# One queue for K and V, and a part of w2 on 64 partitions in eight small transfers

## The chip, the cores and the metric

The kernel runs on one core of a Trainium2 chip. The metric is the device time of the whole program in microseconds (us). Next to it stands the span of one profiled execution, from the first to the last event that the hardware profiler recorded on that core.

The engines of a core have short names here: PE multiplies matrices (PEld loads its weights), DVE and ACT work on vectors and activations, POOL on general operations, SP only issues transfers. "SPq" and "ACTq" are the instruction queues of SP and ACT where they issue a DMA.

## The reference, cut to what matters

One decode step of two branches on the same normalised input, for two sequences (B = 2, one token each, D = 448):

```python
xn = layernorm(x)
q = (xn @ wq) -> 16 heads of 256
k, v = the last 4096 rows of 8 kv heads, each used by 2 query heads
p = softmax(q . k * 256 ** -0.5)
attention = (p . v) @ wo
h = xn @ w1 + b1                                  # 1792 hidden values
dense = (h * tanh(softplus(h))) @ w2
out = x + attention + dense
```

All tensors are bf16. For each pair of a kv head and a sequence, 2 MB of K and 2 MB of V are read once: 64 MB of K and V in all. wq is 3.7 MB, wo 3.7 MB, w1 and w2 1.6 MB each.

## The kernel before

A "head" below is one of the 16 pairs (kv head, sequence); `heads[i]` lists them. The main loop runs over `i` from 0 to 17 and is a software pipeline: at step i it loads K of head i+2 and V of head i, computes the scores of head i, and the values of head i-2 (`KA = 2`).

A K tile holds 128 partitions with 32 key rows each. `turn(s)` (L364) transposes half a K tile on DVE, `scores(s)` (L376) multiplies it on PE with the query block `qdiag`, ACT takes the exponential (L386), `turn_p(s)` (L397) transposes the probabilities on DVE. `values(i)` (L431) multiplies them with V; the last four heads use `values_fixed(i)` (L479), 64 small matmuls per head. `scale_o` (L447) divides by the denominator. After each second head `mix` projects the pair with its slice of wo through `add` (L214) into an accumulator that lives in PSUM to the end. The output is cast by DVE and ACT (L562) and written by one transfer (L563).

The dense branch rides along: `load_dense` loads w1 (L275) and w2 (L280) near the start, `dense_in` computes the hidden values at step 0 (L290, bias L299) and their activation, `dense_out` projects them through w2 at step 1. With 896 hidden values per half of w1 and 128 partitions, there are NF = 7 columns of hidden values for each half. The hidden value number q x 7 + c of a half lies on partition q in column c. b1 has a tile of its own, loaded at the start by ACT.

Queues: SP issues wq, w1, w2, all K tiles, all wo slices, V of the last two heads and the output. ACT issues x, b1 and V of heads 0 to 13. Each engine issues its instructions in program order (`issue_in_order`), a DMA among them; a V load on ACT thus stands between ACT's exponentials.

Buffers: K has 4 tiles, V 5, wo 3. The two parts of wq, w1 and w2 use V tiles before V does. K of head i+2 can be loaded once K of head i-2 has been transposed, V of head i once the values of head i-5 are computed. Besides, the program has eight semaphores for its transfers, used in turn over both queues, and a transfer waits for the one that had its semaphore before.

In the names of the profile, `k`, `v`, `kt`, `pT`, `wo`, `psA` are these tiles; `v` also stands for wq, w1 and w2 in V tiles.

Of the kernel before, what the change touches and what calls it, by code (L numbers as in the profile page):

```python
# [11 lines left out]
BF16 = mybir.dt.bfloat16  # L12
# [22 lines left out]
def kernel(  # L35
# [13 lines left out]
    nc = tc.nc  # L49
    P = 128  # L50
    Q = 32
    NQ = P // Q

    Bsz, Sq, D = A_x.shape
# [6 lines left out]
    F = B_w1.shape[1]  # L61
    T = W // P
    NH = 2
    TH = T // NH
    NX = 2
    NS = D * NX // P
    HW = HqDh // NX
    HF = F // NX
    HH = Hq // NX
    NF = HF // P  # L70
    ND = Dh // P
    NB = Dh // (2 * Q)
    NE = 2
# [13 lines left out]
    consts = ctx.enter_context(tc.tile_pool(name="consts", bufs=1))  # L87
# [8 lines left out]

    x_bf = consts.tile([Bsz, D], BF16)
    nc.scalar.dma_start(out=x_bf[:, :], in_=A_x.flatten_outer_dims())
    b1_sb = consts.tile([1, F], BF16)
    nc.scalar.dma_start(out=b1_sb[:, :], in_=B_b1.rearrange("(o f) -> o f", o=1))  # L100


    def v_tile(n):
        t = v_pool.tile([P, T * Dh], BF16, tag="v", name="v")
        return t[:, 0:n]
# [6 lines left out]
    for lo, hi in ((0, SC), (SC, NS)):  # L112
        w = v_tile((hi - lo) * HW).rearrange("p (s n) -> p s n", n=HW)
# [17 lines left out]
        out=rstd[:], in_=mv[:, 1:2], func=ACT.Sqrt, bias=eps_t[:], scale=1.0  # L131
# [5 lines left out]
    for r in range(2):  # L137
        n = (NS + 1 - r) // 2
        nc.vector.tensor_scalar(  # L139
            out=xn_bf[:, r : NS : 2, :, :],  # L140
# [12 lines left out]
    for b4 in range(NB):  # L153
        rows = slice(b4 * Q, (b4 + 1) * Q)
        for j in range(NQ):
            nc.vector.tensor_copy(
                out=spread[rows, b4, j * Q : (j + 1) * Q], in_=ident[rows, rows]
# [3 lines left out]
    for j in range(1, NQ):  # L161
        nc.vector.tensor_tensor(
            out=hsel, in0=hsel, in1=ident[:, j * Q : (j + 1) * Q : HS], op=ALU.add
# [5 lines left out]
    for i in range(NW):  # L169
        t = consts.tile([P, NB * NE, P], BF16, name=f"qdiag{i}")  # L170
# [5 lines left out]
    for s in range(NS):  # L176
# [7 lines left out]
        out=odd[:],  # L184
        in_=ident[:].rearrange("p (u o) -> p o u", o=2),
# [4 lines left out]
    for par in range(2):  # L190
        for x in range(NX):
            which = (par + x) % 2
            nc.vector.tensor_scalar(
                out=xs[:, par : NS : 2, x, :],
# [14 lines left out]
    def part(n):  # L209
        return psA[n // 2][n * Q : n * Q + Bsz, :]  # L210

    def add(lhsT, w, start=False, stop=False):
        for n in range(NO):
            nc.tensor.matmul(  # L214
                part(n),
                lhsT=lhsT,
                rhs=w[:, n * DO : (n + 1) * DO],
                start=start,
                stop=stop,
                tile_position=(0, n * Q),  # L220
                skip_group_check=True,
            )
# [45 lines left out]


    act_bf = consts.tile([P, NF, NX, Bsz], BF16)  # L270
    dense = {}

    def load_dense():
        dense["w1"] = v_tile(NS * HF).rearrange("p (s n) -> p s n", s=NS)
        nc.sync.dma_start(  # L275
            out=dense["w1"],
            in_=B_w1.rearrange("r (x n) -> (r x) n", x=NX).rearrange("(p s) n -> p s n", s=NS),
        )
        dense["w2"] = v_tile(NX * NF * D).rearrange("p (x c d) -> p x c d", x=NX, c=NF)
        nc.sync.dma_start(  # L280
            out=dense["w2"], in_=B_w2.rearrange("(x q c) d -> q x c d", x=NX, q=P)
        )

    def dense_in():
        w1_v = dense.pop("w1").rearrange("p s (q c) -> p s c q", c=NF)
        b1_v = b1_sb[:].rearrange("o (x q c) -> o x c q", x=NX, c=NF)
        hT_ps = ps_m.tile([P, NF, NX, Bsz], FP32, tag="m", name="hT_ps")
        for c in range(NF):
            for s in range(NS):
                nc.tensor.matmul(  # L290
                    hT_ps[:, c, :, :].rearrange("p x b -> p (x b)"),
                    lhsT=w1_v[:, s, c, :],
                    rhs=xs[:, s, :, :].rearrange("p x b -> p (x b)"),
                    start=(s == 0),
                    stop=False,
                    skip_group_check=True,
                )
            for x in range(NX):
                nc.tensor.matmul(  # L299
                    hT_ps[:, c, x, :],  # L300
                    lhsT=b1_v[:, x, c, :],
                    rhs=ones[:, :],
                    start=False,
                    stop=True,
                    skip_group_check=True,
                )
        shape = [P, NF, NX, Bsz]
        h_sb = consts.tile(shape, FP32, name="h_sb")
        nc.vector.tensor_copy(out=h_sb[:], in_=hT_ps[:])
        u_sb = consts.tile(shape, FP32, name="u_sb")  # L310
        nc.scalar.activation(out=u_sb[:], in_=h_sb[:], func=ACT.Exp)
        t_sb = consts.tile(shape, FP32, name="t_sb")
        nc.vector.scalar_tensor_tensor(
            out=t_sb[:], in0=u_sb[:], scalar=2.0, in1=u_sb[:], op0=ALU.add, op1=ALU.mult
        )
        den = consts.tile(shape, FP32, name="den_sb")
        nc.vector.tensor_scalar(
            out=den[:], in0=t_sb[:], scalar1=2.0, scalar2=None, op0=ALU.add
        )
        nc.vector.reciprocal(out=den[:], in_=den[:])  # L320
        nc.vector.tensor_tensor(out=t_sb[:], in0=t_sb[:], in1=den[:], op=ALU.mult)
        nc.vector.tensor_tensor(out=act_bf[:], in0=h_sb[:], in1=t_sb[:], op=ALU.mult)

    def dense_out():
        w2_sb = dense.pop("w2")
        for x in range(NX):
            for c in range(NF):
                add(act_bf[:, c, x, :], w2_sb[:, x, c, :])


    NSTEP = len(heads) * NH
# [3 lines left out]
    def load_k(i):  # L335
        kvh, b = heads[i]
        t = k_pool.tile([P, T * Dh], BF16, tag="k", name="k")
        nc.sync.dma_start(  # L338
            out=t[:], in_=A_k_cache[b, kvh, s0:Sk, :].rearrange("(p t) d -> p (t d)", p=P)
        )  # L340
        k_t[i] = t

    def load_v(i, queue, cuts=(0, T)):
        kvh, b = heads[i]
        t = v_tile(T * Dh).rearrange("p (t d) -> p t d", t=T)
        vin = A_v_cache[b, kvh, s0:Sk, :].rearrange("(p t) d -> p t d", p=P)
        for lo, hi in zip(cuts, cuts[1:]):
            queue.dma_start(out=t[:, lo:hi, :], in_=vin[:, lo:hi, :])
        v_t[i] = t

    def load_wo(kvh, parts=1):
        w = wo_pool.tile([P, rep, ND * D], BF16, tag="wo", name="wo")
        r0 = kvh * rep * Dh
        win = A_wo[r0 : r0 + rep * Dh, :].rearrange("(h p c) d -> p h (c d)", h=rep, p=P)
        for u in range(parts):
            hs = slice(u * rep // parts, (u + 1) * rep // parts)
            nc.sync.dma_start(out=w[:, hs, :], in_=win[:, hs, :])
        wo_t[kvh] = w

    def turn(s):  # L360
        kt = kt_pool.tile([P, TH * Dh], BF16, tag="kt", name="kt")
        i, half = divmod(s, NH)
        k = k_t[i] if half < NH - 1 else k_t.pop(i)
        nc.vector.transpose(  # L364
            out=kt[:].bitcast(FP32),
            in_=k[:, half * TH * Dh : (half + 1) * TH * Dh].bitcast(FP32),
        )
        kt_t[s] = kt
# [131 lines left out]
    NK = len(heads)  # L500
    KA = 2

    load_k(0)
    load_dense()
    load_k(1)
    project()
# [5 lines left out]
    def close(i):  # L512
        if i < NK - NFIX:
            finish(i)
        kvh, b = heads[i]
        if b == Bsz - 1:
            mix(kvh)

    for i in range(NK + KA):
        if i + 2 < NK:  # L520
            load_k(i + 2)
        if i < NK:
            if i < NK - 2:
                load_v(i, nc.scalar)
            elif i < NK - 1:
                load_v(i, nc.sync)
            else:
                load_v(i, nc.sync, (0, T // 2, 3 * T // 4, T))
            kvh, b = heads[i]
            if b == Bsz - 1:  # L530
                load_wo(kvh, parts=1 if i < NK - 1 else 2)
            for half in range(NH):
                s = i * NH + half
                if s + 1 < NSTEP:
                    turn(s + 1)
                scores(s)
                if s >= 1:
                    turn_p(s - 1)
                if s == NSTEP - 1:
                    turn_p(s)  # L540
                if half == 0 and i > KA:
                    close(i - KA - 1)
            if i + 2 < NK:
                build_q(i + 2)
        if i == NK:
            close(i - KA - 1)
        if i == 0:
            dense_in()
        if i == 1:
            dense_out()  # L550
        if i >= KA:
            if i - KA < NK - NFIX:
                values(i - KA)
            else:
                values_fixed(i - KA)
        if i >= NK:
            close(i - KA)
# [37 lines left out]
```

The softmax here doesn't subtract the row's maximum and nothing guards it: scores larger than these inputs give would overflow.

## Time and profile before

| | us |
|---|---|
| three runs | 193.58, 194.19, 196.42 |
| median | 194.19 |
| the profiled execution's own time | 193.58 |
| its span | 191.8 |
| PE busy (share of the span) | 146.1 (76%) |
| DVE busy | 113.5 (59%) |
| ACT busy | 32.5 (17%) |
| POOL busy | 27.1 (14%) |

The transfers read 77.67 MB from HBM. SP's queue (q1) carried 48.30 MB, ACT's (q10) 29.37 MB; their packets took 59.8% and 35.8% of the time of 16 DMA engines.

How to read the views: the page cuts the span into 40 slices of 4.8 us and gives the busy share of each as a digit. A row of the timeline has start, duration, engine, line, operation, output and input, count, and in brackets how long the engine had been idle and what ended that. A row of the windows has the stretch, its length, then for each engine its busy time and the number of instructions, then the granted clock of PE, the mean busy share of the DMA engines, and GB/s.

DVE waits 45.2 us in all for K tiles (12 waits, the longest 8.7), which is its largest wait.

### The profile page before, as it was taken

To read this page: it belongs to the slowest core of one execution; us is meant where nothing else is said; L and a number is where in the kernel's file an instruction comes from. 1 tells how busy PE (TensorE), PEld (TensorE's weight loads), DVE (VectorE), ACT (ScalarE), POOL (GpSimd) and SP (SyncE) were. 2 spreads that over 40 slices of the span, in tenths; PEclk is the share of its full clock that TensorE was granted. 3 is DMA by queue.
4 is the path that set the end of the run, shared out by engine and by line. 5 is a ranking of instruction groups with operands and counts; after the bars stand their busy time and mean duration, and the time that the engine had idled before them with its cause. 6 is when DMAs were issued, how large, how long until landed. Compare 5 with 4: busy or idle time off the path is not lost.

```text
span 191.8 us, 2945 instructions
## 1 busy us (share of the span) xinstructions
PE 146.1 (76%) x1158; PEld 71.8 (37%) x1158; DVE 113.5 (59%) x195; ACT 32.5 (17%) x82; POOL 27.1 (14%) x139
## 2 busy tenths in 40 slices
PE   0104299389997089998997599978996699869893
PEld 0004238224443034353442243434352244326482
DVE  7800540699940575686923939393918575676731
ACT  2300011011222011122122111220221112211201
POOL 8000433003303002030302021300230030000000
PEclk9999999657999855999999969996999789997985
DMA  6999999999999999999999999999999999999940
GB/s 222 425 429 442 414 428 436 434 434 410 444 424 427 424 433 421 434 427 422 434 431 434 420 431 437 420 434 422 432 431 434 420 429 432 437 418 426 406 173 4
DMA packets 7816, 77.85 MB, mean 406 GB/s; under 512 B 758, under 2 KB 2810, under 8 KB 3323
## 3 DMA queue, kind: packets, MB, share of 16 engines
q1 hardware_dynamic: 5780, 48.30, 59.8%
q10 hardware_dynamic: 2022, 29.37, 35.8%
q8 instruction: 9, 0.15, 0.3%
q14 instruction: 5, 0.03, 0.0%
HBM read 77.67 MB, written 0.00 MB: 405 GB/s over the span
## 4 chain that ended last, share of the span: by engine, by line
DMA 68%; PE 18%; DVE 10%; SPq 1%; issue 1%; ACT 0%; ACTq 0%; DVEq 0%
DMA k<-in_A_k_cache_dram 54%; DMA v<-in_B_w_dram 14%; PE sc L376 9%; DVE kt L364 7%; PE o L431 4%; PE q L479 3%; DVE pT L397 1%; PE psA L214 1%; PE q L460 1%; PE den L414 1%; DVE oT L447 1%; SPq L114 0%; ACT p L386 0%; SPq L275 0%; SPq L338 0%
## 5 line engine op out<-in xcount | busy, mean ns | idle before, releaser
L364 DVE STREAM_TRANSPOSE kt<-k 128x2048 f32<-128x2048 f32 x32 | 73.4, 2295 | 45.2 <-DMA k<-in_A_k_cache_dram 45.2
L376 PE MATMUL sc<-kt,qdiag 128*128 128x512 bf16 x256 | 75.5, 446 | 17.7 <-DVE kt L364 17.0
L376 PEld LDWEIGHTS <-qdiag 128*128 128x128 bf16 x256 | 25.2, 107 | 58.8 <-issue 35.0
L431 PE MATMUL o<-v,pT 128*4 128x512 bf16 x192 | 43.6, 380 | 0.0
L264 POOL COPY qdiag<-qrep 32x8 bf16<-32x8 bf16 x128 | 23.1, 213 | 129.0 <-PE sc L376 109.4
L386 ACT ACTIVATE p<-sc 128x512 bf16<-128x512 f32 x32 | 19.1, 597 | 102.3 <-PE sc L376 100.3
L431 PEld LDWEIGHTS <-pT 128*4 128x4 bf16 x192 | 15.8, 87 | 22.0 <-issue 0.3
L397 DVE STREAM_TRANSPOSE pT<-p 128x512 bf16<-128x512 bf16 x32 | 21.5, 672 | 1.1 <-ACT p L386 1.1
L439 ACT COPY o_sb<-o 4x512 f32<-4x512 f32 x12 | 6.9, 574 | 36.7 <-PE o L431 36.7
L235 PE MATMUL qT_ps<-xs,v 128*128 128x4 bf16 x112 | 3.3, 166 | 9.7 <-DMA v<-in_A_wq_dram 6.9
L214 PE MATMUL psA<-wo,oT 128*2 128x112 bf16 x128 | 3.6, 249 | 8.9 <-DVE oT L447 8.9
L460 PEld LDWEIGHTS q<-ident_f,o_sb 4*128 4x128 f32 x48 | 6.6, 206 | 5.5 <-issue 5.5
L414 PEld LDWEIGHTS den<-sums,ones_f 128*128 128x128 f32 x32 | 6.8, 217 | 3.1 <-issue 1.3
L460 PE MATMUL q<-ident_f,o_sb 4*128 4x4 f32 x48 | 7.6, 261 | 0.0
L462 DVE COPY osum<-q 128x4 f32<-128x4 f32 x12 | 1.9, 159 | 9.4 <-PE q L460 9.4
L479 PEld LDWEIGHTS <-v 128*128 128x128 bf16 x256 | 7.4, 100 | 0.0
L479 PE MATMUL q<-pT,v 128*128 128x2 bf16 x256 | 7.2, 164 | 0.0
L235 PEld LDWEIGHTS <-v 128*128 128x128 bf16 x112 | 3.1, 104 | 9.9 <-DMA v<-in_A_wq_dram 7.0
L244 DVE CAST qT<-qT_ps 128x64 bf16<-128x64 f32 x1 | 0.2, 224 | 10.3 <-PE qT_ps L235 10.3
L386 ACT ACTIVATION_READ_ACCUMULATOR p<-sc 128x1 f32 x32 | 6.2, 194 | 0.0
L214 PEld LDWEIGHTS <-oT 128*2 128x2 bf16 x128 | 1.9, 92 | 9.6 <-DVE oT L447 9.6
L177 PE MATMUL xnT_ps<-ident,xn_bf 2*128 2x2 bf16 x7 | 0.5, 165 | 6.3 <-DVE xn_bf L139 6.3
(52 smaller groups left out, 51.8 us busy)
## 6 DMA issues: line engine op xcount, KB each, us to landing
k<-in_A_k_cache_dram SPq DMA_DIRECT2D x16, 2048.0 KB, 31.8
v<-in_A_v_cache_dram ACTq DMA_DIRECT2D x14, 2048.0 KB, 13.8
v<-in_B_w_dram SPq DMA_DIRECT2D x2, 1568.0 KB, 25.8
wo<-in_A_wo_dram SPq DMA_DIRECT2D x7, 448.0 KB, 33.0
v<-in_A_wq_dram SPq DMA_DIRECT2D x1, 2048.0 KB
v<-in_A_v_cache_dram SPq DMA_DIRECT2D x1, 2048.0 KB, 33.5
v<-in_A_wq_dram SPq DMA_DIRECT2D x1, 1536.0 KB, 15.7
v<-in_A_v_cache_dram SPq DMA_DIRECT2D x1, 1024.0 KB, 22.9
```

Source lines behind the costliest of these rows:

```text
L214: nc.tensor.matmul(part(n), lhsT=lhsT, rhs=w[:, n * DO : (n + 1) * DO], start=start, stop=stop, tile_position=(0, n * Q), skip_group_check ...
L235: nc.tensor.matmul(qT_ps[:, hh, e, :], lhsT=wq_v[s][:, hh, e, :], rhs=xs[:, s, :, :].rearrange("p x b -> p (x b)"), start=(s == 0), stop=( ...
L264: nc.gpsimd.tensor_copy(out=tv[rows, :, e, j * Q : (j + 1) * Q : HS], in_=qrep[rows, :, h0 : h0 + rep, e, x, b],)
L364: nc.vector.transpose(out=kt[:].bitcast(FP32), in_=k[:, half * TH * Dh : (half + 1) * TH * Dh].bitcast(FP32),)
L376: nc.tensor.matmul(psc[:], lhsT=qdiag[i % NW][:, n * NE + e, :], rhs=ktv[:, n, e, :, :], start=(n == 0 and e == 0), stop=(n == NB - 1 and ...
L386: nc.scalar.activation(out=p_sb[:], in_=psc[:].rearrange("p t c -> p (t c)"), func=ACT.Exp, scale=scale, accum_out=state["rs", i][:, s % N ...
L397: nc.vector.transpose(out=pT[:], in_=p_t.pop(s)[:])
L414: nc.tensor.matmul(den[:], lhsT=ones_f[:], rhs=state.pop(("sums", i))[:], start=True, stop=True)
L431: nc.tensor.matmul(po[:], lhsT=pT_t[i * NH + half][:, uh * NP * Q : (uh + 1) * NP * Q : HS], rhs=v[:, u * NP : (u + 1) * NP, :].rearrange( ...
L439: nc.scalar.copy(out=o_sb[:], in_=po[:])
L460: nc.tensor.transpose(pqv[:, u, c, :], ov[:, u, c, :], ident_f[0:NR, 0:NR])
L479: nc.tensor.matmul(po[:, c, :], lhsT=vv[:, t, c, :], rhs=pTv[:, th, 0:Q:HS], start=(t == 0 and c == 0), stop=(t == T - 1), skip_group_chec ...
```

## The change

V loads of all heads are issued by SP, directly after K of head i+2. ACT keeps x and b1.

The hidden values are laid out differently: 6 columns of 128 partitions and 2 columns of 64 partitions (NA = 6, NF = 8) for each half. The rows of w2 that belong to the two short columns have a tile of their own, `w2_rest`, on 64 partitions: 3584 bytes on each, 229 KB in all. It is loaded by eight transfers of eight rows with a step of four partitions, one after V of each of heads 0 to 7, by SP. Its part of the projection runs at step 11 (`dense_rest`) and no longer at step 1. The main part of w2 keeps 5376 of 6272 bytes per partition and half. `hT_ps` is set to zero before the dense input, since two columns fill only 64 partitions. b1 is loaded by ACT into a spare part of the w1 tile.

```diff
-    NF = HF // P
+    PW = P // 2
+    NA = HF // P - 1
+    NF = NA + (HF - P * NA) // PW
...
-    b1_sb = consts.tile([1, F], BF16)
-    nc.scalar.dma_start(out=b1_sb[:, :], in_=B_b1.rearrange("(o f) -> o f", o=1))
...
+    w2_rest = consts.tile([PW, NX, NF - NA, D], BF16)
+    def hidden(c):
+        if c < NA:
+            return slice(0, P), slice(c, P * NA, NA)
+        return slice(0, PW), slice(P * NA + c - NA, HF, NF - NA)
+    w2_in = B_w2.rearrange("(x f) d -> x f d", x=NX)
...
+        w = v_tile(NS * HF + F)
+        dense["w1"] = w[:, 0 : NS * HF].rearrange("p (s n) -> p s n", s=NS)
+        dense["b1"] = w[0:1, NS * HF : NS * HF + F]
...
+        nc.scalar.dma_start(out=dense["b1"], in_=B_b1.rearrange("(o f) -> o f", o=1))
...
-            out=dense["w2"], in_=B_w2.rearrange("(x q c) d -> q x c d", x=NX, q=P)
+            out=dense["w2"],
+            in_=w2_in[:, 0 : P * NA, :].rearrange("x (q c) d -> q x c d", q=P),
...
+    def load_rest(u):
+        q0, j = divmod(u, 4)
+        rows = slice(q0 * Q + j, (q0 + 1) * Q, 4)
+        rest = w2_in[:, P * NA : HF, :].rearrange("x (q c) d -> q x c d", q=PW)
+        nc.sync.dma_start(out=w2_rest[rows, :, :, :], in_=rest[rows, :, :, :])
...
     def dense_in():
+        nc.vector.memset(hT_ps[:], 0.0)
         for c in range(NF):
+            rows, cols = hidden(c)
             for s in range(NS):
                 nc.tensor.matmul(
-                    hT_ps[:, c, :, :].rearrange("p x b -> p (x b)"),
-                    lhsT=w1_v[:, s, c, :],
+                    hT_ps[rows, c, :, :].rearrange("p x b -> p (x b)"),
+                    lhsT=w1[:, s, cols],
...
+    def dense_rest():
+        for x in range(NX):
+            for c in range(NA, NF):
+                add(act_bf[0:PW, c, x, :], w2_rest[:, x, c - NA, :])
...
-            if i < NK - 2:
-                load_v(i, nc.scalar)
-            elif i < NK - 1:
-                load_v(i, nc.sync)
-            else:
-                load_v(i, nc.sync, (0, T // 2, 3 * T // 4, T))
+            load_v(i, (0, T) if i < NK - 1 else (0, T // 2, 3 * T // 4, T))
             kvh, b = heads[i]
+            if i < PW // 8:
+                load_rest(i)
...
+        if i == 11:
+            dense_rest()
```

More of the change, by code (lines that the diff above doesn't have):

```diff
@@ L270 @@
     act_bf = consts.tile([P, NF, NX, Bsz], BF16)
+    w2_rest = consts.tile([PW, NX, NF - NA, D], BF16)
     dense = {}
+    def hidden(c):
[3 more added lines that the diff above has]
+    w2_in = B_w2.rearrange("(x f) d -> x f d", x=NX)
     def load_dense():
-        dense["w1"] = v_tile(NS * HF).rearrange("p (s n) -> p s n", s=NS)
+        w = v_tile(NS * HF + F)
+        dense["w1"] = w[:, 0 : NS * HF].rearrange("p (s n) -> p s n", s=NS)
+        dense["b1"] = w[0:1, NS * HF : NS * HF + F]
         nc.sync.dma_start(
@@ L278, in load_dense @@
         )
-        dense["w2"] = v_tile(NX * NF * D).rearrange("p (x c d) -> p x c d", x=NX, c=NF)
+        nc.scalar.dma_start(out=dense["b1"], in_=B_b1.rearrange("(o f) -> o f", o=1))
+        dense["w2"] = v_tile(NX * NA * D).rearrange("p (x c d) -> p x c d", x=NX, c=NA)
         nc.sync.dma_start(
-            out=dense["w2"], in_=B_w2.rearrange("(x q c) d -> q x c d", x=NX, q=P)
-        )
+            out=dense["w2"],
+            in_=w2_in[:, 0 : P * NA, :].rearrange("x (q c) d -> q x c d", q=P),
+        )
+    def load_rest(u):
[3 more added lines that the diff above has]
+        nc.sync.dma_start(out=w2_rest[rows, :, :, :], in_=rest[rows, :, :, :])
     def dense_in():
-        w1_v = dense.pop("w1").rearrange("p s (q c) -> p s c q", c=NF)
-        b1_v = b1_sb[:].rearrange("o (x q c) -> o x c q", x=NX, c=NF)
+        w1, b1 = dense.pop("w1"), dense.pop("b1")
         hT_ps = ps_m.tile([P, NF, NX, Bsz], FP32, tag="m", name="hT_ps")
+        nc.vector.memset(hT_ps[:], 0.0)
         for c in range(NF):
+            rows, cols = hidden(c)
             for s in range(NS):
                 nc.tensor.matmul(
-                    hT_ps[:, c, :, :].rearrange("p x b -> p (x b)"),
-                    lhsT=w1_v[:, s, c, :],
+                    hT_ps[rows, c, :, :].rearrange("p x b -> p (x b)"),
+                    lhsT=w1[:, s, cols],
                     rhs=xs[:, s, :, :].rearrange("p x b -> p (x b)"),
@@ L299, in dense_in @@
                 nc.tensor.matmul(
-                    hT_ps[:, c, x, :],
-                    lhsT=b1_v[:, x, c, :],
+                    hT_ps[rows, c, x, :],
+                    lhsT=b1[:, x * HF + cols.start : x * HF + cols.stop : cols.step],
                     rhs=ones[:, :],
@@ L326, in dense_out @@
         for x in range(NX):
-            for c in range(NF):
+            for c in range(NA):
                 add(act_bf[:, c, x, :], w2_sb[:, x, c, :])
+    def dense_rest():
+        for x in range(NX):
+            for c in range(NA, NF):
+                add(act_bf[0:PW, c, x, :], w2_rest[:, x, c - NA, :])
     NSTEP = len(heads) * NH
@@ L341, in load_k, with load_v @@
         k_t[i] = t
-    def load_v(i, queue, cuts=(0, T)):
+    def load_v(i, cuts=(0, T)):
         kvh, b = heads[i]
@@ L347, in load_v @@
         for lo, hi in zip(cuts, cuts[1:]):
-            queue.dma_start(out=t[:, lo:hi, :], in_=vin[:, lo:hi, :])
+            nc.sync.dma_start(out=t[:, lo:hi, :], in_=vin[:, lo:hi, :])
         v_t[i] = t
```

## The prediction

> **What bounds the kernel now.** I read the page's slices and chain first, then the DMA issues, then the busy time in short windows near the end, then the timeline of the end.
>
> ```profile
> DMA  6999999999999999999999999999999999999940
> GB/s 222 425 429 442 414 428 436 434 434 410 444 424 427 424 433 421 434 427 422 434 431 434 420 431 437 420 434 422 432 431 434 420 429 432 437 418 426 406 173 4
> DMA 68%; PE 18%; DVE 10%; SPq 1%; issue 1%; ACT 0%; ACTq 0%; DVEq 0%
> ```
>
> From the second slice to the thirty-eighth (4.8 to 182 us) the 16 DMA engines are full. No compute engine is: PE is busy 76%, DVE 59%. So the time is a stream of 77.85 MB, plus a short start, plus what runs on after the stream. The windows say where each ends (columns: busy time and count on PE, PEld, DVE, ACT, POOL; granted clock; DMA share; GB/s):
>
> ```profile
> 28.00:38.00 10.00, 6.83 (x73) 5.33 (x72) 2.98 (x3) 1.11 (x4) 1.46 (x8) 0.86 1.02 438
> 98.00:108.00 10.00, 8.23 (x41) 3.70 (x39) 4.85 (x7) 1.95 (x5) 1.45 (x8) 1.00 1.01 433
> 172.00:183.00 11.00, 10.29 (x153) 6.24 (x152) 7.67 (x11) 2.07 (x6) 0.00 (x0) 0.86 1.01 418
> 183.50:184.00 0.50, 0.30 (x17) 0.20 (x17) 0.15 (x1) 0.00 (x0) 0.00 (x0) 1.00 0.67 260
> 184.00:184.50 0.50, 0.50 (x20) 0.50 (x13) 0.08 (x1) 0.00 (x0) 0.00 (x0) 1.00 0.62 237
> 184.50:185.00 0.50, 0.50 (x26) 0.50 (x23) 0.09 (x1) 0.00 (x0) 0.00 (x0) 1.00 0.35 133
> 185.00:185.50 0.50, 0.50 (x26) 0.50 (x23) 0.00 (x0) 0.00 (x0) 0.00 (x0) 0.85 0.00 0
> ```
>
> The last load lands at **185.0**: a third of the engines is through by 183.5, a third works until the last half microsecond. So the engines differ by about 1.5 us at the end. The span ends at 191.8, 6.8 us later, and the timeline shows what fills this:
>
> ```profile
> 164.82 2.31 DVE L364 STREAM_TRANSPOSE kt<-k 128x2048 f32<-128x2048 f32 x1 [3.02 <-DMA k<-in_A_k_cache_dram]
> 173.34 2.31 DVE L364 STREAM_TRANSPOSE kt<-k 128x2048 f32<-128x2048 f32 x1 [1.93 <-DMA k<-in_A_k_cache_dram]
> 181.43 1.79 PE L479 MATMUL q<-pT,v 128*128 128x2 bf16 x64
> 184.24 1.81 PE L479 MATMUL q<-pT,v 128*128 128x2 bf16 x64
> 186.35 1.85 PE L479 MATMUL q<-pT,v 128*128 128x2 bf16 x64
> 188.45 0.54 PE L214 MATMUL psA<-wo,oT 128*2 128x112 bf16 x16 [0.26 <-DVE oT L447]
> 189.02 0.56 DVE L562 CAST res<-psA 2x112 bf16<-2x112 f32 x2 [0.62 <-PE psA L214]
> 189.64 0.33 SPq L563 DMA_DIRECT2D out_dram<-res  x1
> ```
>
> The last two K tiles (heads 14 and 15) land at 164.8 and 173.3. After them PE and DVE work nearly without a gap, and the last projection starts at 188.45, 3.4 us after all data is there. The end is set by **when the last K tiles land** and the work that follows from them in order; not by the end of the stream. From head 14's K to the last projection it is 188.45 - 164.82 = 23.6 us.
>
> Why so late? The issues (median us to landing in the last column):
>
> ```profile
> k<-in_A_k_cache_dram SPq DMA_DIRECT2D x16, 2048.0 KB, 31.8
> v<-in_A_v_cache_dram ACTq DMA_DIRECT2D x14, 2048.0 KB, 13.8
> ```
>
> V from ACT lands in 13.8 us, K from SP in 31.8: a V tile, issued late, shares the engines with K tiles issued long before, and overtakes them. V of head 13 goes out at 158.91 and lands ahead of much that SP has queued.
>
> **What the Trainium skill says.** "DMA: Bandwidth & Descriptors", section "Issuing engines are not separate DMA queues": transfers issued by sync, scalar and gpsimd run on the same 16 engines and interleave; several issuers save only issue time. The trace agrees: 438 GB/s in 28 to 38 us, where ACT issued nothing after 4.9 us, against 433 in 98 to 108 with both queues at work. "Perfetto Trace Analysis", section "Roofline", puts a single core's ceiling at about 435 GB/s for the 16 engines; these windows sit on it. "DMA: Bandwidth & Descriptors", section "Why a DMA increments its semaphore by 16 and not by 1": a transfer uses the largest number of engines up to 16 that divides its slowest dimension, and takes the lowest-numbered ones. So eight rows use engines 0 to 7; no run shown has such a transfer.
>
> **The change, part by part.**
>
> *V of heads 0 to 13 moves from ACT to SP.* Bytes and rate stay. ACT loses 14 issues of 0.34 us (17% busy: worth nothing). SP gains 14 issues of about 0.33 and eight small ones, some 8 us over the span; its queue is idle most of the time. What changes is order: one queue gives k(i+2), v(i), small transfer or wo, in turn. After the K of head 15 the queue then holds v13, wo6, v14, v15, wo7 = 3 x 2.10 + 2 x 0.46 = 7.21 MB; at the 418 GB/s of 172 to 183 us that is 17.2 us. After the K of head 14 it holds v12 and k15 too, 11.40 MB, 27.3 us. With the stream's end still at 185.0, K of head 15 lands at 167.8 (5.5 earlier) and K of head 14 at 157.7 (7.1 earlier). The same 23.6 us of work from there would reach the last projection at 181.3: before its data.
>
> So **the stream's end is late next**. wo7's second half lands last, at 185.0; V's last quarter 0.46 MB before it, 1.1 us, at 183.9. The quarter needs 16 of the 64 matmuls of L479 (1.85/4 = 0.46) and 0.4 us for the scaling: 184.8. Then the last projection waits for wo7: 185.0, 0.1 for the signal (my estimate), 8 of 16 matmuls 0.27, casts to the output's issue 189.64 - 189.02 = 0.62, output 191.80 - 189.64 = 2.16. Sum **188.2, against 191.8: -3.6 us**.
>
> *Waits now in SP's line.* v(i) waits for the values of head i-5, behind it stand k(i+3) and everything later. Also every transfer waits for the one eight places ahead of it in the program (eight semaphores in turn). With k, v and the small transfer, and wo every second head, v(i) goes out when k(i) has landed, at which time v(i-2), k(i+1), v(i-1), k(i+2) are queued: four times 4.9 us. The values of head i-5 are computed two heads earlier. A hold-up under some 19 us therefore leaves no engine idle: 0.
>
> *Start.* The first V (2 MB) no longer shares the engines with wq, so projection and scores begin up to 4.9 us earlier; in a full stream this is worth nothing at the end.
>
> *w2 in two parts.* The main part shrinks on each of 16 engines by 8 rows x 1792 B = 14.3 KB; eight engines get 8 x 3584 B = 28.7 KB in its place. Net +14.3 KB on eight engines, -14.3 KB on the others, at 433/16 = 27 GB/s: **plus or minus 0.53 us**. If the late engines of 183.5 to 185.0 are all among the relieved ones, the stream ends 0.5 earlier; if among the loaded ones, 0.5 later. The page doesn't name engines. I take 0 and keep both ends.
>
> *Dense input.* 72 matmuls in place of 63, and a memset first. 63 took 4.6 us (29.7 to 34.3), so +0.7 us. The memset (nearest row: 146 ns for the copy of the same 128 rows, L309) stands on DVE behind the transpose of head 1's first half, so PE now waits for head 1's K there. In the new order that lands after 10.85 MB (25.2 us at 430 GB/s, from 2.3 us on, since the first slice moves half a slice's load), at about 27.5 in place of 35.0, so PE is through at about 36, before the 37.5 at which the next scores began. Free, the stream covers it. If the cover failed, it costs 0.8 us.
>
> *Dense output.* 16 projections of 16 ns (0.89/56) move to step 11, eight fewer at step 1: +0.26 us beside waits for K of 3 us. b1 goes into the w1 tile: one row, 3.5 KB, early.
>
> **The rivals.**
>
> *Compute still sets the end* (10%). SP's line holds K back behind V, so the last K lands no earlier than 173. For: every K issue now has a V wait ahead of it. Against: four tiles in the queue. Time as before, 193.6 to 194.2.
>
> *Small transfers on one engine* (6%, the slower side). If the eight rows go to one engine and not eight, it carries 229 KB more: at 27 GB/s 8.5 us less 0.5 saved. Every later transfer waits for it; the stream ends at 193.0, the span at 196.2, the time at 198 to 198.6. The point: with two engines (four rows each) the extra is 115 KB less 14, 3.7 us, and cancels the gain; with one the kernel is slower. Against: the skill's rule.
>
> *SP starves the engines* (6%). If values fall over 19 us behind, each microsecond more is lost at the end; 5 us would give about 195.5. Against: SP's longest wait on PE is 0.5 us now.
>
> *The relieved engines are the late ones and the gain is larger* (18%): stream's end 184.5, 187.6, time about 189.9.
>
> **How the numbers follow.** The profiled run took 193.58, 1.78 over its span; the median shown is 194.19, 0.6 above it. -3.6 on the median gives 190.6; with the small lean of the fourth case I say **190.5**. My main case (60%) has 189.6 to 191.8. Two per cent of 194.19, about what a measurement tells from no change, is 190.3: just at my forecast, so faster and same are near even: 0.42 and 0.46; slower 0.12 for the one-engine case and the worse half of the others. Range 189.0 to 194.3: from the larger gain with a quick run up to no gain.
>
> **What would show it.** Right: K landing 16 to 18 us ahead of the stream's end; waits for K on DVE gone after about 170; the last matmuls of L479 and the last projection waiting for DMA; the output issued about 1 us after the last load, not 4.6. Wrong: a DMA slice under 9 in the middle; L479 still running without waits past the last load; a stream's end beyond 185.6; the DMA share trailing at one sixteenth.

## The result, and the profile after

The changed kernel takes 191.04 us (median of 6 runs, 190.90 to 191.16) against 194.00 for the kernel before beside it: a ratio of **0.9854, interval 0.9834 to 0.9875**. That is 3.0 us less, clear of the noise though under 2%. One of the six runs of the kernel before, 196.42 us, was slowed, as some runs of these kernels are; the ratio here and all ratios below leave such runs out, and without it the kernel before has 193.82 and the gain is 2.8 us. The forecast was 190.5, with 189.0 to 194.3 as the range. The profiled execution took 190.99 us with a span of 189.2, 2.6 less than before.

First the page after: the DMA slices, the rates, the chain by engine, and the issues of K and V (last column: median us to landing).

```profile
DMA  6999999999999999999999999999999999999990
GB/s 215 427 440 418 431 433 426 431 431 415 436 426 429 430 422 436 432 433 400 441 443 420 440 422 426 426 433 419 444 426 426 430 426 435 433 426 416 417 384 19
DMA 84%; DVE 9%; PE 3%; SPq 1%; issue 0%; ACT 0%; ACTq 0%
k<-in_A_k_cache_dram SPq DMA_DIRECT2D x16, 2048.0 KB, 25.7
v<-in_A_v_cache_dram SPq DMA_DIRECT2D x15, 2048.0 KB, 26.2
```

The stream looks as it did: full from the second slice on, at the same rates. No slice in the middle is under 9, so one queue starves nothing. The issues show what moved: K needed 31.8 us to land and V 13.8; now both need 26. And the chain that ends last has changed hands: DMA holds 84% of it in place of 68%, PE 3% in place of 18%.

Next the timeline of the end, after: each row is one group of like instructions, with what it had waited for in brackets.

```profile
159.09 2.31 DVE L389 STREAM_TRANSPOSE kt<-k 128x2048 f32<-128x2048 f32 x1 [3.42 <-DMA k<-in_A_k_cache_dram]
168.82 2.31 DVE L389 STREAM_TRANSPOSE kt<-k 128x2048 f32<-128x2048 f32 x1 [3.15 <-DMA k<-in_A_k_cache_dram]
183.74 0.59 PE L504 MATMUL q<-pT,v 128*128 128x2 bf16 x16 [0.21 <-DMA v<-in_A_v_cache_dram]
184.96 0.58 PE L504 MATMUL q<-pT,v 128*128 128x2 bf16 x16 [0.64 <-DMA v<-in_A_v_cache_dram]
185.80 0.60 PE L214 MATMUL psA<-wo,oT 128*2 128x112 bf16 x16 [0.26 <-DVE oT L472]
186.42 0.56 DVE L586 CAST res<-psA 2x112 bf16<-2x112 f32 x2 [0.68 <-PE psA L214]
187.04 0.29 SPq L587 DMA_DIRECT2D out_dram<-res  x1
```

K of heads 14 and 15 can be transposed at 159.1 and 168.8, where it was 164.8 and 173.3. The work that follows from K no longer reaches the end: the last matmuls of L504 stop for V. V's last quarter sets the end, and behind it stand 0.84 us of matmuls and scaling, 0.6 of projection, 0.6 of casts and 2.2 of output. The last projection (L214) waits for the scaled values `oT`, not for a transfer.

And the windows of the end, after (DMA share and GB/s are the last two columns):

```profile
184.00:184.50 0.50, 0.32 (x13) 0.24 (x9) 0.00 (x0) 0.00 (x0) 0.00 (x0) 0.50 0.82 300
184.50:185.00 0.50, 0.04 (x1) 0.04 (x2) 0.00 (x0) 0.00 (x0) 0.00 (x0) 0.50 0.28 104
185.00:185.50 0.50, 0.50 (x16) 0.46 (x16) 0.00 (x0) 0.00 (x0) 0.00 (x0) 0.50 0.16 61
185.50:186.00 0.50, 0.24 (x10) 0.18 (x9) 0.17 (x1) 0.00 (x0) 0.00 (x0) 0.50 0.02 7
```

Before, the share was 0.62, 0.35 and 0.00 in the first three. More engines now work together up to 184.5, but a few (0.16 of 16 is two or three) go on past 185.5, half a microsecond longer.

So two things stand side by side: the end moved from the compute to the stream, and the stream itself ends at least 0.5 us later. Theory: V's queue does the first, and is the whole gain; the split of w2 does the second, and is a loss. Rivals: the split evens out the engines and brings the gain; or the order of the last heads alone matters.

### The profile page after: what moved, and what is told of

It is laid out like the page before. It is cut to its first block, busy times and chain, and to the rows that moved or that the text cites. A ratio compares the mean times of both kernels' runs of the same rounds, so it can differ in the third digit from the quotient of the medians.

```text
span 189.2 us, 2989 instructions
## 1 busy us (share of the span) xinstructions
PE 143.1 (76%) x1175; PEld 71.4 (38%) x1175; DVE 113.6 (60%) x196; ACT 32.5 (17%) x82; POOL 27.2 (14%) x139
## 4 chain that ended last, share of the span: by engine, by line
DMA 84%; DVE 9%; PE 3%; SPq 1%; issue 0%; ACT 0%; ACTq 0%
DMA k<-in_A_k_cache_dram 70%; DMA v<-in_A_v_cache_dram 14%; DVE kt L389 7%; PE hT_ps L310 2%; DVE pT L422 1%; PE hT_ps L319 1%; SPq L114 0%; PE psA L214 0%; PE q L504 0%; SPq L286 0%; SPq L292 0%; SPq L363 0%; DVE den_sb L340 0%; ACTq L614 0%; ACT u_sb L331 0%
## 5 line engine op out<-in xcount | busy, mean ns | idle before, releaser
L401 PE MATMUL sc<-kt,qdiag 128*128 128x512 bf16 x256 | 70.4, 422 | 11.9 <-DVE kt L389 11.8
L456 PE MATMUL o<-v,pT 128*4 128x512 bf16 x192 | 44.3, 384 | 0.0
L401 PEld LDWEIGHTS <-qdiag 128*128 128x128 bf16 x256 | 24.0, 103 | 49.5 <-issue 21.5
L214 PE MATMUL psA<-wo,oT 128*2 128x112 bf16 x128 | 3.2, 219 | 9.9 <-DVE oT L472 9.9
L310 PE MATMUL hT_ps<-xs,v 128*128 128x4 bf16 (+1 forms) x56 | 4.0, 190 | 8.1 <-DVE hT_ps L306 8.1
L504 PE MATMUL q<-pT,v 128*128 128x2 bf16 x256 | 7.6, 165 | 1.9 <-DMA v<-in_A_v_cache_dram 1.8
L504 PEld LDWEIGHTS <-v 128*128 128x128 bf16 x256 | 7.5, 101 | 2.2 <-DMA v<-in_A_v_cache_dram 2.2
L310 PEld LDWEIGHTS <-v 128*128 128x128 bf16 (+1 forms) x56 | 3.3, 144 | 8.6 <-issue 8.5
L214 PEld LDWEIGHTS <-oT 128*2 128x2 bf16 x128 | 1.6, 81 | 10.7 <-DVE oT L472 10.6
L439 PE MATMUL den<-sums,ones_f 128*128 128x2 f32 x32 | 5.5, 242 | 0.0
```

The costliest lines, as they stand in the source:

```text
L214: nc.tensor.matmul(part(n), lhsT=lhsT, rhs=w[:, n * DO : (n + 1) * DO], start=start, stop=stop, tile_position=(0, n * Q), skip_group_check ...
L310: nc.tensor.matmul(hT_ps[rows, c, :, :].rearrange("p x b -> p (x b)"), lhsT=w1[:, s, cols], rhs=xs[:, s, :, :].rearrange("p x b -> p (x b) ...
L401: nc.tensor.matmul(psc[:], lhsT=qdiag[i % NW][:, n * NE + e, :], rhs=ktv[:, n, e, :, :], start=(n == 0 and e == 0), stop=(n == NB - 1 and ...
L439: nc.tensor.matmul(den[:], lhsT=ones_f[:], rhs=state.pop(("sums", i))[:], start=True, stop=True)
L456: nc.tensor.matmul(po[:], lhsT=pT_t[i * NH + half][:, uh * NP * Q : (uh + 1) * NP * Q : HS], rhs=v[:, u * NP : (u + 1) * NP, :].rearrange( ...
L504: nc.tensor.matmul(po[:, c, :], lhsT=vv[:, t, c, :], rhs=pTv[:, th, 0:Q:HS], start=(t == 0 and c == 0), stop=(t == T - 1), skip_group_chec ...
```

## The experiments

Each ran beside the kernel before on the same chip. Four chips were used: one for the first three below and the 64-row transfer, one for the last four (the changed kernel and V on SP alone again, more on eight engines, the smaller last piece), one for the last eight heads and the first run of 16 rows, one for its second run. The kernel before takes 193.3 to 193.6 us (median) on all four, and V on SP alone 190.49 and 190.50 on two of them; times that differ by half a microsecond are compared only within a chip.

**V on SP alone.** The kernel before, one word changed:

```diff
             if i < NK - 2:
-                load_v(i, nc.scalar)
+                load_v(i, nc.sync)
```

> The kernel before with V of all heads on SP and nothing else changed (w2 whole, b1 at the start). If the order of the last K tiles is the cause, this alone brings the gain: K of head 15 lands near 168.5, the last projection waits for V's last quarter and wo, span 188.7 to 189.7, ratio 0.983 to 0.988. If the split of w2 brings the gain (DMA engines evened out), this stays at the time before, ratio 0.995 to 1.005.

Measured: 190.49 us, ratio 0.9867 (0.9834 to 0.9900), span 188.6. The queue alone brings the gain. Its issues, the windows of the end, and the timeline of the end:

```profile
k<-in_A_k_cache_dram SPq DMA_DIRECT2D x16, 2048.0 KB, 31.4
v<-in_A_v_cache_dram SPq DMA_DIRECT2D x15, 2048.0 KB, 34.7
```

```profile
184.00:184.50 0.50, 0.24 (x9) 0.25 (x10) 0.00 (x0) 0.00 (x0) 0.00 (x0) 0.50 0.60 229
184.50:185.00 0.50, 0.35 (x13) 0.26 (x10) 0.12 (x1) 0.00 (x0) 0.00 (x0) 0.50 0.57 205
185.00:185.50 0.50, 0.40 (x16) 0.28 (x16) 0.05 (x1) 0.00 (x0) 0.00 (x0) 0.50 0.00 0
```

```profile
168.41 2.31 DVE L364 STREAM_TRANSPOSE kt<-k 128x2048 f32<-128x2048 f32 x1 [3.12 <-DMA k<-in_A_k_cache_dram]
184.26 0.59 PE L479 MATMUL q<-pT,v 128*128 128x2 bf16 x16 [0.62 <-DMA v<-in_A_v_cache_dram]
185.10 0.60 PE L214 MATMUL psA<-wo,oT 128*2 128x112 bf16 x16 [0.26 <-DVE oT L447]
```

K of head 15 can be used at 168.4, as the first expectation says. K still needs 31.4 us from issue to landing, as before the change, but V needs 34.7 and no longer overtakes it: what counts is the order in which tiles land, not the time that one spends in the queue. With w2 whole the stream ends at 185.0, as before the change, and V's last quarter is there 0.7 us sooner than in the changed kernel.

**The split alone.** The changed kernel, V of heads 0 to 13 back on ACT:

```diff
-            load_v(i, (0, T) if i < NK - 1 else (0, T // 2, 3 * T // 4, T))
+            load_v(
+                i,
+                nc.scalar if i < NK - 2 else nc.sync,
+                (0, T) if i < NK - 1 else (0, T // 2, 3 * T // 4, T),
+            )
```

> The changed kernel with V of heads 0 to 13 back on ACT, so the split of w2 and its eight transfers alone. If the order is the cause, the end is again set by the last K tiles: span 191.3 to 192.3, ratio 0.997 to 1.003. If the split brings the gain, ratio near 0.985. If the eight transfers or the dense input's wait for the memset cost something that the new order hides, ratio above 1.003.

Measured: 193.70 us, ratio 1.0034 (1.0013 to 1.0055). No gain; a small loss, just over the bound of the third expectation (1.003), which lies inside the interval. Little of it is in the part that the profiler sees: the median span is 191.6 against 191.5 for the kernel before, while time and span differ by 2.1 us here and by 1.8 there. Where the 0.3 us outside the span come from stays open. Two rows of its timeline show the old end again, K of head 15 late and the last projection after 188:

```profile
173.49 2.31 DVE L389 STREAM_TRANSPOSE kt<-k 128x2048 f32<-128x2048 f32 x1 [2.52 <-DMA k<-in_A_k_cache_dram]
188.21 0.54 PE L214 MATMUL psA<-wo,oT 128*2 128x112 bf16 x16 [0.26 <-DVE oT L472]
```

**Only the last four heads on SP.** The kernel before, with the bound moved:

```diff
-            if i < NK - 2:
+            if i < NK - 4:
                 load_v(i, nc.scalar)
```

> The kernel before with only V of heads 12 and 13 moved to SP as well (heads 0 to 11 stay on ACT). If only what stands ahead of the last two K tiles counts, this gives nearly the whole gain: K of head 15 lands by 169, ratio 0.983 to 0.990. If the order must hold from the start (start of the stream, ACT's freed queue), less than half of it: ratio 0.993 to 1.000.

Measured: 191.97 us, ratio 0.9927 (0.9907 to 0.9947): half the gain, between the two expectations. That is the median of a wide spread, 190.45 to 193.14: four of the 22 runs lie between 190.45 and 190.86 and have the whole gain or nearly so. The profiled run is the longest, 193.14, so its rows show how a run loses the gain, and not the median. The first transpose of the K tile of heads 12, 13, 14 and 15 in its timeline, and the last projection:

```profile
146.50 2.31 DVE L364 STREAM_TRANSPOSE kt<-k 128x2048 f32<-128x2048 f32 x1 [7.30 <-DMA k<-in_A_k_cache_dram]
153.60 2.30 DVE L364 STREAM_TRANSPOSE kt<-k 128x2048 f32<-128x2048 f32 x1
164.63 2.30 DVE L364 STREAM_TRANSPOSE kt<-k 128x2048 f32<-128x2048 f32 x1
172.55 2.30 DVE L364 STREAM_TRANSPOSE kt<-k 128x2048 f32<-128x2048 f32 x1
188.00 0.54 PE L214 MATMUL psA<-wo,oT 128*2 128x112 bf16 x16 [0.26 <-DVE oT L447]
```

Read the brackets: DVE waits 7.3 us for K of head 12 and for no K after it. The transposes of heads 13 to 15 come late although their data is there. The compute from head 12 on takes 188.00 - 146.50 = 41.5 us, about 10 us a head, as long as the stream needs for a head (4.19 MB at 430 GB/s, 9.8 us). So in this run a delay of K does not heal within three heads: it is carried to the end. V of heads 9 to 11, still on ACT, are issued at 118.26, 126.19 and 135.52, all after K of head 12, and share the engines with it.

**The last eight heads on SP.** The same with `NK - 8`. (The expectation names head 13; by the rows above it was head 12.)

> The kernel before with V of heads 8 to 13 moved to SP (heads 0 to 7 stay on ACT). With only heads 12 and 13 moved, half the gain came, and K of head 13 was the last that DVE waited for. If what counts is that no K of the last five or six heads is overtaken, this gives the whole gain: ratio within 0.0015 of V on SP alone, 0.987. If the order at the start counts as well, about 0.990.

Measured: 190.85 us (190.38 to 191.09), ratio 0.9864 (0.9833 to 0.9895): by the ratio the gain of V on SP alone (0.9867), on another chip, and by the spans too (188.6 to 188.9 against 188.6 to 188.8). The order has to hold for the last eight heads or fewer; at the start it is worth nothing that these runs resolve.

**The short part of w2 in one transfer on 16 engines.** The changed kernel, with

```diff
     def load_rest(u):
-        q0, j = divmod(u, 4)
-        rows = slice(q0 * Q + j, (q0 + 1) * Q, 4)
+        rows = slice(0, PW)
...
-            if i < PW // 8:
+            if i == 0:
                 load_rest(i)
```

> The changed kernel with the 64 rows of the short part of w2 in one transfer of 64 rows after V of head 0, so on all 16 engines in place of eight. If the eight loaded engines are the late ones, the stream ends up to 0.5 us earlier, ratio 0.982 to 0.985. If the relieved ones were the late ones before, it ends later, ratio 0.986 to 0.990. If which engine is late is chance, the changed kernel's 0.985 within 0.001.

Measured: 191.67 us, ratio 0.9924 (0.9900 to 0.9949), slower than every expectation. Most of the reason isn't at the end but where the transfer runs. Its windows from 37 to 41 us:

```profile
37.00:38.00 1.00, 1.00 (x12) 0.82 (x12) 0.16 (x1) 0.00 (x0) 0.00 (x0) 0.50 0.98 340
38.00:39.00 1.00, 1.00 (x4) 0.29 (x3) 0.64 (x4) 0.23 (x1) 0.00 (x0) 0.50 1.35 301
39.00:40.00 1.00, 1.00 (x4) 0.43 (x3) 0.93 (x4) 0.00 (x0) 0.00 (x0) 0.50 0.70 268
40.00:41.00 1.00, 1.00 (x4) 0.14 (x1) 1.00 (x1) 0.00 (x0) 0.00 (x0) 0.50 1.03 369
```

320 GB/s on average, where the two profiles of the changed kernel have 425 and 437 in the same 4 us: 0.42 to 0.47 MB, 1.0 to 1.1 us of stream, lost to a transfer of 0.23 MB. The time of this run says nothing on which engines are late, since it carries this cost.

**Four transfers of 16 rows.** To part the two: rows `slice(u, PW, 4)` after V of heads 0 to 3, again on 16 engines.

> The changed kernel with the short part of w2 in four transfers of 16 rows (16 engines, one row each, step of four partitions) after V of heads 0 to 3, in place of eight of eight rows. The one transfer of 64 rows lost about 1 us of the stream. If that was 16 engines writing to 64 partitions, each of these dips too, a quarter of a microsecond each, and the time is that of the 64-row kernel (0.7 us above the changed kernel). If it was the 64-row transfer itself, there is no dip, the load of all engines is even and the time is 0.5 us below the changed kernel, that of V on SP alone; if it then stays above that, the rest is the dense branch's own cost.

Measured: 190.96 us (four runs, 190.81 to 191.09), ratio 0.9873 (0.9840 to 0.9906), near the changed kernel's, which ran on other chips. Beside it on its own chip stand the last eight heads on SP, with w2 whole: their spans are 188.6 to 188.9, those of this kernel 189.0 to 189.3. So even loads did not bring the half microsecond back. The same kernel on another chip:

> Four transfers of 16 rows once more, for an undisturbed trace. If writing 64 partitions from 16 engines is what slowed the one transfer of 64 rows, the stretch of about 2 us after each of the four (near 38, 48, 58 and 69 us) moves about 0.1 MB less than the changed kernel's 430 GB/s would, and the last load lands at 185.3 or later. If not, no dip, and the last load lands at 185.0 as with V on SP alone.

Measured: 191.23 us, ratio 0.9881 (0.9848 to 0.9914). Its trace has a stretch from 58 to 72 us with all packets slowed, so only the first two transfers can be read. Five microseconds around each, this kernel first, then the changed kernel's second profile:

```profile
37.00:42.00 5.00, 4.48 (x19) 1.71 (x19) 3.85 (x8) 0.92 (x3) 0.00 (x0) 0.51 1.01 421
47.00:52.00 5.00, 4.30 (x21) 2.02 (x22) 4.96 (x8) 1.36 (x4) 1.50 (x8) 1.00 1.01 415
```

```profile
37.00:42.00 5.00, 4.47 (x20) 1.81 (x21) 3.71 (x8) 0.85 (x3) 0.00 (x0) 0.57 1.02 432
47.00:52.00 5.00, 4.21 (x22) 1.98 (x22) 4.96 (x8) 1.38 (x4) 1.49 (x8) 1.00 0.99 412
```

A dip of 11 GB/s at the first and none at the second: nothing like 110 GB/s over 4 us. The 64-row transfer is slow and not 16 engines as such; why stays open. What even loads are worth stays open too: a dip like the first at each of the four transfers would cost 0.5 us (my estimate, 4 x 55 KB at 430 GB/s), as much as an even load could win.

**The changed kernel and V on SP alone, side by side.**

> The changed kernel itself, once more, to stand beside the next kernels on one chip. Ratio 0.983 to 0.988. If the split of w2 adds something to V on SP, it lies below the kernel with V on SP alone by 0.3 us or more; if it costs, above by as much.

> V of all heads on SP alone, w2 whole, once more on the same chip as the changed kernel. Theory (V's queue is all of it): within 0.3 us of the changed kernel. Rival (the split evens out the engines and is worth up to 0.5 us): 0.3 to 0.6 us above it. Rival (the split costs): 0.3 to 0.6 us below it.

Measured: 190.98 us (190.87 to 191.18; ratio 0.9889, 0.9858 to 0.9921) for the changed kernel, 190.50 (190.39 to 190.84; ratio 0.9867, 0.9835 to 0.9899) with w2 whole. The ranges of the runs don't meet, if only just (190.84 and 190.87), and the medians differ by 0.48: the split costs 0.5 us.

**More on the eight engines.** The changed kernel, with four more transfers of eight rows after V of head 0; they read part of w2 a second time, and nothing uses it:

```diff
+    def load_again():
+        t = dense.pop("again")
+        main = w2_in[0, 0 : P * NA, :].rearrange("(q c) d -> q (c d)", q=P)
+        for j in range(4):
+            rows = slice(j, Q, 4)
+            nc.sync.dma_start(out=t[rows, :], in_=main[rows, :])
```

> The changed kernel with four more transfers of eight rows (5376 bytes a row, 21.5 KB more on each of eight engines, read again from w2 into an unused part of a tile). If the eight loaded engines are the late ones, the stream ends 0.8 us later and the time with it (0.8 us above the changed kernel). If the others are late, less than 0.3 us. If lateness is chance, about 0.4 us.

Measured: 191.73 us (191.66 to 191.92), ratio 0.9930 (0.9903 to 0.9956): 0.75 above the changed kernel, where full weight was 0.8. The end of the stream in its windows:

```profile
185.00:185.50 0.50, 0.09 (x4) 0.00 (x1) 0.00 (x0) 0.00 (x0) 0.00 (x0) 0.50 0.33 128
185.50:186.00 0.50, 0.29 (x10) 0.29 (x11) 0.00 (x0) 0.00 (x0) 0.00 (x0) 0.50 0.21 79
186.00:186.50 0.50, 0.30 (x12) 0.21 (x9) 0.16 (x1) 0.00 (x0) 0.00 (x0) 0.50 0.11 43
```

The stream ends near 186.4: the engines that trail in the changed kernel are among those that get the eight rows, and what is put on them counts in full. 172 KB over one engine would have been 6.4 us and over 16 engines 0.4; 0.75 is eight.

The traces hold a closer view, which the pages don't print: the landing events of each transfer. A tile of 128 rows leaves 16 of them; a transfer of eight rows leaves one at its issue and eight when its data lands. I read one event as one engine. Those of the last transfer, the second half of wo's last slice, in us:

| | early | between | last | mean of all 16 |
|---|---|---|---|---|
| V on SP alone | seven, 183.52 to 184.44 | none | nine, 185.15 to 185.30 | 184.71 |
| changed kernel | two, 183.06 and 183.53 | eleven, 184.57 to 185.12 | three, 185.72 to 186.00 | 184.78 |
| more on eight | two, 183.06 and 183.60 | eleven, 184.64 to 185.95 | three, 186.44 to 186.78 | 185.20 |

The second profiles of the first two kernels have the same groups. The means of the first two differ by 0.07 us, so the split hardly slows the stream; it spreads its end. This fits nine late engines of which the split loads three and relieves six: the three come 0.5 to 0.7 us later, the six end with the middle. The 64-row kernel and the second run of 16 rows, which load all engines alike, end in seven and nine again, though their times did not come below the changed kernel's.

**A smaller last piece.** V on SP alone, V of head 15 cut at seven eighths as well: `(0, T // 2, 3 * T // 4, 7 * T // 8, T)`.

> V of all heads on SP, w2 whole, and V of the last head cut at seven eighths too, so that only 8 of 64 matmuls follow its last piece. The last stretch of matmuls took 0.59 us; half of it goes: 0.3 us below V on SP alone. If the last projection waits for wo and not for V, nothing.

Measured: 190.66 us (190.52 to 190.84), ratio 0.9872 (0.9841 to 0.9903): no gain. A row of its timeline:

```profile
184.27 0.97 PE L479 MATMUL q<-pT,v 128*128 128x2 bf16 x31 [0.77 <-issue]
```

The last 31 matmuls run in one go, after an idle stretch of PE for which the profile shows no wait. The second profile of V on SP alone has such a stop too. So this run did not have the case that it was built for, eight matmuls alone behind the last piece, and whether a smaller piece could help stays open.

## Why the prediction was right

- *What bounds the kernel.* Right. The stream is full throughout, and before the change the last K tiles and the compute behind them set the end. But "the last two K tiles" was too narrow: with only V of heads 12 and 13 moved, half the gain came, and in the profiled run of that kernel compute, at some 10 us a head, carried a late K of head 12 to the end.
- *V's queue.* Right. K of head 15 was forecast at 167.8 and could be used at 168.8, head 14 at 157.7 and 159.1. The stream's end was late next, as said. K of head 15 lands 17 us ahead of it, within the 16 to 18 named as a sign. V on SP alone gives ratio 0.9867, the split alone 1.0034.
- *The sum of the end.* 188.2 forecast, 189.2 measured. The term that was mis-sized is V's last quarter, forecast at 183.9, usable at 184.96: 1.06 late. 0.7 of it is against V on SP alone (184.26), thus the split; the other 0.36 is there with w2 whole. Most of that is probably the way from the last byte to its signal, taken as 0.1 for wo and as nothing for V: in V on SP alone the last packets of wo end at 185.0 and the last landing event stands at 185.30. The work after it agrees in sum by luck: from V at 183.9 to 188.2 it was 4.3, measured 4.2, but the forecast let the last projection wait for wo's last slice and counted half of it (0.27), while it waited for V's scaling and took 0.6 behind it. "The last projection waiting for DMA" was named as a sign and did not come.
- *The time.* 190.5 against 191.04 is closer than the span, also by luck: 188.2 plus the 1.8 us between span and time would be 190.0. The forecast took its 3.6 us from a median of three runs that lay 0.6 above the profiled one.
- *w2 in two parts.* The bound held: plus or minus 0.53 was stated, and the loss is 0.5, the upper end. I took 0 and gave the gain at the other end 18%. A stream's end beyond 185.6 was named as a sign of being wrong, and the changed kernel stands on that line. The reading behind it was off: a DMA share of 0.35 in the last half microsecond is a mean, not a third of the engines. By the landing events of the kernel before, ten of 16 engines end within 0.8 us (184.57 to 185.34), and no choice of eight can relieve ten.
- *Dense input.* The memset held PE back, as worked out: 8.1 us of waiting ahead of L310, which then ran from 32.8 to 37.5 us, later than the 36 forecast. The stream stayed full over it, so it is covered. Its share in the 0.5 us was not measured alone; but PE waits for V at the end, so a delay at 37 us is not on the path there.
- *The rivals.* Compute at the end: no, L504 waits for V. SP starving the engines: no, its longest wait on PE is 0.7 us and no slice is under 9. Small transfers on one engine: no, the extra load cost what eight engines would need, and eight landing events follow each small transfer. Late engines among the relieved: by the landing events six of nine were, and it did not help, since the other three were not.

Engines that a page can't name are the weak spot. By the rule of the Trainium skill ("DMA: Bandwidth & Descriptors", section "Why a DMA increments its semaphore by 16 and not by 1") a transfer of eight rows runs on eight engines, the lowest-numbered ones. The price of the extra load (0.75 us) and the eight landing events of each small transfer agree with eight; which numbers they have, no run here shows.

## What to carry to other kernels

Where the stream is full, look at what still has to be computed when its last bytes land, and at which transfers land too early: one queue that keeps the order of use was worth 1.3% here with not a byte less. When the last stage is computing, a late tile some heads back can be its cause, if compute needs as long for a tile as the stream. Before putting load on a few DMA engines to even them out, find out how many are late and which: here nine of 16 ended together, 14 KB more on each of eight engines and 14 KB less on the others cost half a microsecond, and V on SP with w2 whole beats both kernels at 190.5 us.

## What the runs showed that I had not expected

A transfer of 64 rows (two pieces of 1792 bytes each) on 16 engines held the stream at 320 GB/s for 4 us (425 and 437 over the same stretch in the changed kernel) and cost more than four of 16 rows or eight of eight rows with the same bytes. And two queues do not share the engines by age: V, issued on the second queue, landed in 13.8 us while K tiles issued before it took 31.8.
